# Three output weight pieces converted beside expert 0's first half; VectorE's side work per step set by expert width; first input sums two per step

## The chip, the cores and the metric

The kernel runs on one core of one Trainium2 chip. Its engines are TensorE (PE: matrix products; PEld: the loading of its weights), VectorE (DVE), ScalarE (ACT), GpSimd (POOL) and SyncE (SP, which here only issues DMAs). Each works through its own list of instructions in the order in which the program was written; between engines, semaphores hold an instruction until what it reads is there or what it overwrites has been read. The metric is the device time of one execution in microseconds (us), less is better.

## The reference

Three layers follow one another. The numbers of one feed the next.

```
# 1: gated linear attention, 4 batches x 8 heads, 768 steps, head size 48
f = 1 / (1 + exp(-f_logit))
for t in range(768):
    state = f[t] * state + outer(k[t], v[t])
    y[t] = q[t] @ state
# 2: x = y as (3072, 384); 8 experts (384 -> 1024 -> 384), one for each token
logits = normalised(x) @ normalised(expert_emb).T / tau
expert_idx = argmax(logits); gate = softmax(logits)[expert_idx]
out[mask] = gate * (relu(x[mask] @ w1[e]) @ w2[e])         # for each expert e
# 3: "moe2": w_a, w_b 384 -> 1536, w_out 1536 -> 384
result = ((x @ w_a) * (x @ w_b)) @ w_out
```

## The kernel before, in words

**Numbers in two parts.** A product is made with rounded operands, each kept as a high part (`Copy` on ScalarE) and a low part (raw minus high, a subtraction on GpSimd or VectorE), and three products of high and low are summed. So every weight and every intermediate costs ScalarE one pass and VectorE or GpSimd another.

**Stages.** The scan of the attention runs in 24 groups (`g`) until about 120 us; its inputs q, k, f come through four buffers `qkf0` to `qkf3`. Tokens are scattered to memory by expert (`slots`) with indirect DMAs on GpSimd's queue. Then the first 224 tokens of expert 0 are worked off in the **early stage** (`early_h`, `early_y`, `early_split`, lines 521 to 541, 127 to 145 us) while the rest of the routing is counted on VectorE. Then comes the **expert loop**, `for s in range(64)` with `e, j = divmod(s, 8)`: step s makes one eighth of expert e's hidden layer (`h_part`, products on lines 1212 to 1214, split into `hh` on ScalarE, line 1235, and `hl` on VectorE, line 1236) and adds the eighth before it to the output (`y_part(s - 1)`, line 1255). An expert is 224, 448, 432, 416, 408, 400, 392 or 384 tokens wide (e = 0 to 7). In steps j = 3 to 5 the rows of the next expert are transposed (`x_turn`, TensorE line 1202, then ScalarE line 1205 and VectorE line 1206). The loop ends at about 381 us; after it layer 3 runs in "visits" (lines 1461 to 1494) to about 808 us.

**Side work in the expert loop.** Layer 3's weights come in 64-bit form and are made into 32-bit floats, 18 pieces of 128 x 768 in `conv()`: load (line 925), `Abs` on ScalarE (948), four bit operations on VectorE (950, 951, 954 and 957 or 987). The six pieces of `w_out` are then split (ScalarE 963, GpSimd 964) and stored to the scratch array `wost` (SP, line 969); the twelve of `w_a` and `w_b` are summed into combined blocks in `combine()` (VectorE 999, 1000; ScalarE 1032; GpSimd or VectorE 1035) and stored to `wst` (SP, line 1055). The order of pieces (`waiting`) is three of `w_out`, six of `w_a`, six of `w_b`, three of `w_out`. The experts' own weights are split as they come (`w_more`: ScalarE 886 and 892, two thirds of the low part on GpSimd and one third on VectorE, 887 and 895). From step 58 on the first input sums of layer 3 are made too (`x_first`: VectorE 1347 and 1355, ScalarE 1360).

**What sets the order.** Nothing reorders instructions when the program runs: each engine's list is the order in which the loop calls its parts. `prep_run(s, us)` hands out side work in each step until the costs that its generators yield (estimates written in the code, in us of VectorE) have used up `us`: 1.4 in expert 0, 2.1 later. A step calls `h_part`, `prep_run`, `w_more`, `x_turn` and `y_part(s - 1)` in that order, so VectorE's `hl` of a step stands behind the side work of the step before it.

**Buffers.** When the first stage ends, its pools are closed (`actx.close()`), and the space is given to new ones: `big` (9216 columns, which holds the six buffers `part[0]` to `part[5]` of `conv`), the hidden layer's `hid` pool (`hh`, `hl`), and `yT`. `rows1`, the rows of expert 1, lies in `yT[2]`. They are loaded by SP (line 463), as the first of SP's DMAs after the early stage; behind it on SP stand `w2` weights of an expert (line 130), the first three loads of `conv` (line 925) and the rows of expert 2.

## Time and profile before

| | |
|---|---|
| median of 3 runs | 813.92 us (813.72 to 816.1) |
| profiled execution, its own time | 815.84 us |
| its span | 813.8 us (so 2.04 us lie around the span) |
| PE busy / PEld busy | 769.0 us (95%) / 738.7 us |
| DVE, ACT, POOL busy | 603.7, 420.5, 411.6 us |
| DMA over the span | 226.82 MB, mean 279 GB/s |
| stages on PE | scan to about 120 us, early stage to 145, expert loop to 381, layer 3 to 808 |

How to read it: the profile's page gives busy times by engine and the span in 40 slices; the waits list what TensorE stood for; a timeline gives the instructions of one engine in order, with the idle time ahead of one and what ended it in brackets. PEclk 1.00 is TensorE's full speed.

### The profile page before, as it was taken

To read this page: it belongs to the slowest core of one execution; us is meant where nothing else is said; L and a number is where in the kernel's file an instruction comes from. 1 tells how busy PE (TensorE), PEld (TensorE's weight loads), DVE (VectorE), ACT (ScalarE), POOL (GpSimd) and SP (SyncE) were. 2 spreads that over 40 slices of the span, in tenths; PEclk is the share of its full clock that TensorE was granted. 3 is DMA by queue.
4 is the path that set the end of the run, shared out by engine and by line. 5 is a ranking of instruction groups with operands and counts; after the bars stand their busy time and mean duration, and the time that the engine had idled before them with its cause. 6 is when DMAs were issued, how large, how long until landed. Compare 5 with 4: busy or idle time off the path is not lost.

```text
span 813.8 us, 16794 instructions
## 1 busy us (share of the span) xinstructions
PE 769.0 (95%) x6354; PEld 738.7 (91%) x6354; DVE 603.7 (74%) x1007; ACT 420.5 (52%) x889; POOL 411.6 (51%) x392
## 2 busy tenths in 40 slices
PE   7899989889999899997899999999999999999995
PEld 5799989878998899986798999999999999999994
DVE  6999995589978956787888557856756765786552
ACT  4899974555556646654345344434434434444331
POOL 6667773352377936874255153445326525343313
PEclk9999999999999999999999999999999999999998
DMA  7999852977689975997997998789889888988881
GB/s 272 308 309 319 247 185 92 293 257 236 186 250 284 310 246 170 256 258 230 342 406 288 338 334 321 278 322 335 299 299 325 316 291 313 336 286 306 336 308 64
DMA packets 83088, 226.82 MB, mean 279 GB/s; under 512 B 10650, under 2 KB 42248, under 8 KB 76728
## 3 DMA queue, kind: packets, MB, share of 16 engines
q1 hardware_dynamic: 79639, 216.10, 78.3%
q0 software_dynamic: 3072, 9.56, 3.0%
q8 instruction: 52, 0.85, 0.4%
q14 instruction: 37, 0.30, 0.1%
q10 hardware_dynamic: 288, 0.02, 0.0%
HBM read 192.95 MB, written 32.70 MB: 277 GB/s over the span
## 4 chain that ended last, share of the span: by engine, by line
PE 40%; DVE 8%; DMA 3%; issue 1%; POOL 1%; ACT 1%; SPq 0%; DVEq 0%; POOLq 0%; ACTq 0%
PE pv L1461 21%; PE pw L1461 5%; PE pq L1492 5%; PE pq L1490 5%; PE pq L1494 5%; DMA w<-wst 3%; DVE a L1355 2%; DVE big L1438 2%; DVE big L1477 2%; DVE big L1471 1%; DVE w L1355 1%; POOL out L1523 0%; POOL big L964 0%; DVE big L1474 0%; PE po L1255 0%
## 5 line engine op out<-in xcount | busy, mean ns | idle before, releaser
L1443 POOL TENSOR_TENSOR w<-big,w 128x512 fp32r<-128x512 f32 x72 | 94.2, 1322 | 173.8 <-ACT w L1442 169.6
L1461 PE MATMUL pv<-w,w 128*128 128x256 f32 x912 | 135.6, 283 | 7.0 <-DMA w<-wst 2.4
L1477 DVE TENSOR_TENSOR big<-big,pv 128x512 f32<-128x512 f32 x144 | 98.2, 682 | 58.5 <-PE pv L1461 58.3
L1461 PEld LDWEIGHTS pv<-w,w 128*128 128x128 f32 x912 | 126.3, 189 | 11.5 <-DVE big L1477 3.8
L1461 PE MATMUL pv<-a,w 128*128 128x256 f32 x816 | 120.3, 281 | 0.6 <-DVE big L1471 0.3
L1461 PEld LDWEIGHTS pv<-a,w 128*128 128x128 f32 x816 | 113.5, 188 | 2.4 <-DVE big L1471 1.4
L895 POOL TENSOR_TENSOR w<-raw,w 128x512 fp32r<-128x512 f32 x48 | 78.5, 1654 | 48.1 <-ACT w L892 45.4
L1494 PE MATMUL pq<-raw,w 128*128 128x384 f32 x288 | 97.2, 338 | 1.6 <-POOL w L1443 1.6
L1490 PE MATMUL pq<-raw,w 128*128 128x384 f32 x288 | 97.4, 338 | 0.0
L1492 PE MATMUL pq<-raw,w 128*128 128x384 f32 x288 | 96.9, 337 | 0.0
L1255 PE MATMUL po<-hh,w 128*128 128x224 f32 (+7 forms) x384 | 82.0, 348 | 7.4 <-ACT hh L1235 6.9
L1471 DVE TENSOR_TENSOR big<-big,pv 128x256 f32<-128x256 f32 x96 | 40.3, 420 | 50.5 <-PE pv L1461 48.7
L1255 PEld LDWEIGHTS po<-hh,w 128*128 128x128 f32 x384 | 67.1, 191 | 10.1 <-ACT hh L1235 7.9
L1438 DVE TENSOR_TENSOR big<-big 128x512 f32<-128x512 f32 x72 | 66.1, 946 | 1.6
L1212 PE MATMUL ph<-a,w 128*128 128x224 f32 (+7 forms) x192 | 66.5, 346 | 0.0
L1214 PE MATMUL ph<-a,w 128*128 128x224 f32 (+7 forms) x192 | 66.3, 345 | 0.0
L1213 PE MATMUL ph<-a,w 128*128 128x224 f32 (+7 forms) x192 | 66.3, 345 | 0.0
L1442 ACT ACTIVATE w<-big 128x512 fp32r<-128x512 f32 x72 | 44.8, 633 | 38.5 <-DVE big L1438 38.5
L1468 ACT ACTIVATE big<-pw 128x256 f32<-128x256 f32 x48 | 18.3, 382 | 77.7 <-PE pw L1461 77.7
L1235 ACT ACTIVATE hh<-ph 128x224 fp32r<-128x224 f32 (+7 forms) x64 | 31.3, 490 | 52.0 <-PE ph L1214 51.8
L1494 PEld LDWEIGHTS pq<-raw,w 128*128 128x128 f32 x288 | 54.3, 189 | 2.2 <-POOL w L1443 2.2
L1490 PEld LDWEIGHTS pq<-raw,w 128*128 128x128 f32 x288 | 54.3, 189 | 0.6 <-ACT w L1442 0.6
(275 smaller groups left out, 1738.2 us busy)
## 6 DMA issues: line engine op xcount, KB each, us to landing
w<-wst SPq DMA_DIRECT2D x49, 1024.0 KB, 7.3
w<-wst SPq DMA_DIRECT2D x49, 896.0 KB, 6.1
raw<-wost SPq DMA_DIRECT2D x72, 384.0 KB, 7.1
raw<-moe_w SPq DMA_DIRECT2D x32, 768.0 KB, 6.8
qkf<-qkf SPq DMA_DIRECT2D x20, 768.0 KB, 5.1
wst<-big SPq DMA_DIRECT2D x21, 512.0 KB, 7.3
vx<-vx SPq DMA_DIRECT2D x24, 192.0 KB
big<-moe_w_out SPq DMA_DIRECT2D x6, 768.0 KB
```

Of the source, the lines that this page charges most:

```text
L895: (G if i < NPOOL else V).tensor_tensor(out=wt[:, 1, f], in0=raw[:, f], in1=wt[:, 0, f].bitcast(F32), op=ALU.subtract)
L1212: T.matmul(out=out, lhsT=wh, rhs=xh, start=first, stop=False)
L1213: T.matmul(out=out, lhsT=wl, rhs=xh, start=False, stop=False)
L1214: T.matmul(out=out, lhsT=wh, rhs=xl, start=False, stop=last)
L1255: T.matmul(out=OS[e][k], lhsT=w[:, j % 4, k * 128:(k + 1) * 128], rhs=x, start=(j == 0 and w is wh and x is hh), stop=(j == FJ - 1 and x i ...
L1438: V.tensor_tensor(out=a, in0=a, in1=b, op=ALU.mult)
L1443: G.tensor_tensor(out=g[:, 1], in0=a, in1=g[:, 0].bitcast(F32), op=ALU.subtract)
L1461: T.matmul(out=out, lhsT=wt, rhs=xt_, start=first and j == 0, stop=j == 2, skip_group_check=True)
L1477: V.tensor_tensor(out=o, in0=o, in1=bank, op=ALU.subtract)
L1490: T.matmul(out=q, lhsT=gh, rhs=wh, start=(f == 0), stop=False)
L1492: T.matmul(out=q, lhsT=gh, rhs=wl, start=False, stop=False)
L1494: T.matmul(out=q, lhsT=gl, rhs=wh, start=False, stop=(f == F2J - 1))
```

## The change

The instructions of TensorE are the same 5901 in the same order. What moves are the lists of the other engines.

1. Three of the six `w_out` pieces (c = 0, 2, 4) are loaded by SP in groups 20, 21 and 22 of the scan into `qkf0`, `qkf1`, `qkf2`, which are free by then (`pre_load`), and converted by `pre()`, a generator that is called by `pre_step` between the parts of the early stage: per piece ScalarE `Abs`, VectorE four operations (max, shift, two bit operations), ScalarE `Copy`, GpSimd subtraction, and two stores to `wost` issued on **GpSimd's** queue. The results lie in `qkf3`, `qkf0`, `qkf1`.
2. `conv` keeps 15 pieces: `w_a`, `w_b`, then three of `w_out`. The first three loads are pieces of `w_a`. The last operation of a `w_a` piece is one of 128 x 3 x 256 instead of three of 128 x 256 (`yT` is one tile now). The late `w_out` results lie in tiles of expert 7's input, and their conversion starts 8 places after the load instead of 3.
3. `rows1` lies in the first columns of `big`.
4. `prep_run` gets `prep_share(s)`, worked out from the expert's width, from what VectorE has in the step anyway, and carries an overdraft to the next step (`debt`). The costs yielded by `conv` and `combine` are changed a little.
5. `w_more(s)` is called ahead of `h_part(s)`, VectorE's third of the weights' low part behind `prep_run`.
6. `x_first` makes two sums a step from s = 57 (three a step from s = 58 before), and one each at the first two places of layer 3.

```
+        pre_to = {0: 3, 2: 0, 4: 1}
+        def pre_load(i):
+            src = I["moe2_w_out"].bitcast(I32).rearrange("(j p) d -> p j d", p=128)[:, 4 * i:4 * i + 2, :]
+            raw = qkf_t[i].rearrange("p c a b -> p (c a b)").bitcast(I32)
+            SP.dma_start(out=raw.rearrange("p (j f) -> p j f", j=2), in_=src)
+        def pre():
+            ct = Bt_all.rearrange("p i a b -> p (i a b)")[:, 0:768]
+            for i in range(3):
+                c = 2 * i
+                ...
+                A.activation(out=ct, in_=r1.bitcast(F32), func=ACTF.Abs)
+                V.tensor_scalar(out=ct, in0=ct, scalar1=C0, scalar2=None, op0=ALU.max)
+                yield
+                V.tensor_scalar(out=ct.bitcast(I32), in0=ct.bitcast(I32), scalar1=3, scalar2=0x3fffffff, ...)
+                yield
+                V.scalar_tensor_tensor(out=r0, in0=r0, scalar=29, in1=ct.bitcast(I32), ...)
+                yield
+                V.scalar_tensor_tensor(out=r0, in0=r1, scalar=-1073741824, in1=r0, ...)
+                to = qkf_t[pre_to[c]].rearrange("p c a b -> p (c a b)").rearrange("p (i j d) -> p i j d", i=2, j=2)
+                src = r0.bitcast(F32).rearrange("p (j d) -> p j d", j=2)
+                A.activation(out=to[:, 0].bitcast(F32R), in_=src, func=ACTF.Copy)
+                G.tensor_tensor(out=to[:, 1].bitcast(F32R), in0=src, in1=to[:, 0], op=ALU.subtract)
+                for h in range(2):
+                    G.dma_start(out=wost[2 * c:2 * c + 2, :, h].rearrange("j p d -> p j d"), in_=to[:, h])
+                yield
...
+            if 20 <= g <= 22:
+                pre_load(g - 20)
...
         early_split(3)
+        pre_step(1)
...
         early_split(7)
+        pre_step(2)
         late_turn()
+        pre_step(1)
         early_y(6)
+        pre_step(2)
...
-        yT = [sp.tile([128, max(sum(CAPS), NT + DM)], F32, name=f"yT{k}") for k in range(KC)]
-        rows1 = yT[2][:, NT - 4 * RW:NT].rearrange("p (j w) -> p j w", j=4)
+        yTs = sp.tile([128, KC, max(sum(CAPS), NT + DM)], F32, name="yT")
+        yT = [yTs[:, k] for k in range(KC)]
+        rows1 = big[:, 0:4 * RW].rearrange("p (j w) -> p j w", j=4)
...
-        waiting = [(w, c) for w in (2, 0, 1, 2) for c in ((0, 2, 4) if w == 2 else range(6))]
-        waiting[-3:] = [(2, 1), (2, 5), (2, 3)]
+        waiting = [(w, c) for w in (0, 1) for c in range(6)] + [(2, 1), (2, 5), (2, 3)]
...
+            us += debt[0]
...
+            debt[0] = min(us, 0)
...
+        def prep_share(s):
+            e, j = divmod(s, FJ)
+            turning = 3 <= j <= 5 and e + 1 < NE
+            us = 18 * max(0.111, 0.000457 * n_of(e)) + (1.0 if turning else 0.0)
+            return PREP * us - 0.56 * (1 + turning + (j == 0)) - 1.2 * len(vlow) - (2.0 if s >= IDS else 0.0)
...
         for s in range(NE * FJ):
             e, j = divmod(s, FJ)
+            w_more(s)
             h_part(s)
...
-            prep_run(s, 1.4 if s < FJ else 2.1)
-            w_more(s)
+            prep_run(s, prep_share(s))
+            while vlow:
+                vlow.pop(0)()
...
-            if s == IDS + 1:
+            if s == IDS:
                 x_more()
-            if s > IDS:
-                for _ in range(3):
+            if s >= IDS:
+                for _ in range(2):
                     next(x_first, None)
```

ScalarE at the end of the early stage, before: `he` are the early halves, `a0` the late rows of expert 0 turned, `sq_junk` the squares of rows, `hh` the hidden layer of step 0.

```order
L525 ACTIVATE he00_155<-u_ps_151 128x224 [waits DVE_49,PE_49]
L525 ACTIVATE he10_157<-y_ps_152 128x224 [waits DVE_49,PE_49]
L501 ACTIVATE a0_88<-u_ps_151 128x224 [waits DVE_49,PE_49]
L501 ACTIVATE a0_88<-ph_2276 128x224 [waits PE_49]
L501 ACTIVATE a0_88<-px_2474 128x224 [waits PE_49]
L541 ACTIVATE rows_84<-kv_2242 128x224 [waits DVE_49,PE_49]
```

ScalarE at the same place now; `Bt` holds the magnitudes, `qkf` the pieces and their high parts.

```order
L568 ACTIVATE Bt_150<-qkf1_147 128x768 [waits DMAHW5_49]
L526 ACTIVATE he00_155<-u_ps_151 128x224 [waits PE_49]
L526 ACTIVATE he10_157<-y_ps_152 128x224 [waits PE_49]
L581 ACTIVATE qkf0_146<-qkf1_147 128x768 [waits DVE_49,Pool_49]
L568 ACTIVATE Bt_150<-qkf2_148 128x768 [waits DMAHW7_49]
L502 ACTIVATE a0_88<-u_ps_151 128x224 [waits PE_49]
L502 ACTIVATE a0_88<-ph_2279 128x224 [waits PE_49]
L502 ACTIVATE a0_88<-px_2497 128x224 [waits PE_49]
L581 ACTIVATE qkf1_147<-qkf2_148 128x768 [waits DVE_49,Pool_49]
L542 ACTIVATE rows_84<-kv_2245 128x224 [waits PE_49]
```

Line 501 before is line 502 now. Behind the third `Abs` stand the late turn and the third `Copy`, and the eviction to `rows` comes behind that. The first `hh` follows after three more instructions.

SP, before, from the load of expert 1's rows (`slots` to `yT2`); DMAHW and DMASW are semaphores of DMAs that SP and GpSimd issued.

```order
L463 DMA yT2_2534<-slots_70 112x1576 [waits DVE_49,DMAHW7_49,PE_49,Pool_49]
L130 ISA
L130 DMA raw_2564<-moe_w2 128x4x384 [waits DMAHW1_49,DMAHW0_49]
L925 DMA big_2525<-moe2_w_out 128x2x768 [waits DMAHW3_49,DMAHW2_49,Pool_49]
L925 DMA big_2525<-moe2_w_out 128x2x768 x2
```

SP at that place now.

```order
L464 DMA big_2555<-slots_70 112x1576 [waits DMASW5_49,DMASW4_49,DMAHW2_49,DMASW3_49,DMAHW3_49,DMASW2_49,DMAHW4_49,DMASW1_49,DMAHW5_49,DMASW0_49,DMAHW7_49,PE_49,Pool_49]
L131 ISA
L131 DMA raw_2592<-moe_w2 128x4x384
L983 DMA big_2555<-moe2_w_a 128x3x512 x2
L983 DMA big_2555<-moe2_w_a 128x3x512 [waits DMAHW6_49]
```

The load of expert 1's rows goes to `big` and waits for six DMAs of GpSimd's queue, which it did not wait for before. The loads behind it are in the same order, with pieces of `w_a` in place of pieces of `w_out`.

VectorE in steps 58 and 59, before: 1236 is `hl`, 999 a combined block, 895 the low part of expert weights, 1347 and 1355 the sums of layer 3's input.

```order
L1236 SCALAR_TENSOR_TENSOR hl<-ph,hh 128x384
L999 TENSOR_TENSOR big<-big 128x512 x2
L1347 TENSOR_TENSOR rows<-yT_2533,yT_2534 128x256
L1347 TENSOR_TENSOR rows<-yT_2532,rows 128x256
L1347 TENSOR_TENSOR rows<-yT_2532 128x256
L1347 TENSOR_TENSOR rows<-rows 128x256
L1355 TENSOR_TENSOR w_66<-rows,w_66 128x256 x2
L1347 TENSOR_TENSOR rows<-yT_2532,yT_2534 128x256
L1236 SCALAR_TENSOR_TENSOR hl<-ph,hh 128x384
L999 TENSOR_TENSOR big<-big 128x512 x2
L895 TENSOR_TENSOR w_65<-raw,w_65 128x512
```

VectorE at the same steps now (1295 is `hl`, 1405 and 1413 the sums, 936 the low part of weights).

```order
L1295 SCALAR_TENSOR_TENSOR hl<-ph,hh 128x384
L1413 TENSOR_TENSOR w_66<-rows,w_66 128x256
L1405 TENSOR_TENSOR rows<-yT 128x256
L1413 TENSOR_TENSOR w_66<-yT,w_66 128x256
L1405 TENSOR_TENSOR rows<-yT,rows 128x256
L1295 SCALAR_TENSOR_TENSOR hl<-ph,hh 128x384
L936 TENSOR_TENSOR w_65<-raw,w_65 128x512
```

The combined blocks are gone from these steps (they are done before step 57), and the sums stand in smaller lots between two `hl`.

## Rows read from the trace of the kernel before

**Rows 1.** The page: busy time by engine, and TensorE's granted clock in 40 slices.
```profile
PE 769.0 (95%) x6354; PEld 738.7 (91%) x6354; DVE 603.7 (74%) x1007; ACT 420.5 (52%) x889; POOL 411.6 (51%) x392
...
PEclk9999999999999999999999999999999999999998
```

**Rows 2.** TensorE's waits: what it waited for, total, times, longest.
```profile
PE po L1255 <- ACT hh L1235: 6.9, 3, 4.0
PE pt L1202 <- DVE a L1206: 5.4, 2, 2.8
PE po L1255 <- DVE hl L1236: 4.6, 4, 1.8
```

**Rows 3.** TensorE's timeline: start, duration, instruction, idle before and what ended it.
```profile
147.02 0.93 PE L1255 MATMUL po<-hh,w 128*128 128x224 f32 x6
...
158.78 0.60 PE L1202 MATMUL pt<-ident,yT 112*128 112x112 f32 x4 [2.67 <-DVE a L1206]
...
260.49 0.83 PE L1255 MATMUL po<-hl,w 128*128 128x416 f32 x3 [1.77 <-DVE hl L1236]
...
283.26 0.71 PE L1202 MATMUL pt<-ident,rows 100*128 100x100 f32 x4 [2.77 <-DVE a L1206]
...
363.69 1.32 PE L1255 MATMUL po<-hh,w 128*128 128x384 f32 x6 [1.90 <-ACT hh L1235]
...
371.14 1.37 PE L1255 MATMUL po<-hh,w 128*128 128x384 f32 x6 [4.03 <-ACT hh L1235]
```

**Rows 4.** SP's timeline: the load of expert 1's rows.
```profile
145.19 0.33 SPq L463 DMA_DIRECT2D yT<-slots  x1
```

**Rows 5.** ScalarE's timeline, early stage and the loop's first steps.
```profile
133.12 0.36 ACT L525 ACTIVATE he<-u_ps 128x224 fp32r<-128x224 f32 x1 [1.53 <-PE u_ps L521]
...
146.63 0.81 ACT L1235 ACTIVATE hh<-ph 128x224 fp32r<-128x224 f32 x2
...
154.85 0.90 ACT L948 ACTIVATE ct<-big 128x768 f32<-128x768 f32 x1 [3.16 <-DMA big<-moe_w_out]
...
161.76 0.90 ACT L963 ACTIVATE big<-big 128x768 fp32r<-128x768 f32 x1 [2.10 <-DVE big L957]
```

**Rows 6.** VectorE's timeline: the bit operations of the first pieces.
```profile
155.79 0.56 DVE L950 TENSOR_SCALAR ct<-ct 128x768 f32<-128x768 f32 x1 [3.67 <-ACT ct L948]
...
158.95 1.78 DVE L954 SCALAR_TENSOR_TENSOR big<-big,ct 128x768 int32<-128x768 int32 x1
160.76 0.96 DVE L957 SCALAR_TENSOR_TENSOR big<-big 128x768 int32<-128x768 int32 x1
...
163.48 1.54 DVE L950 TENSOR_SCALAR ct<-ct 128x768 f32<-128x768 f32 x1 [0.93 <-ACT ct L948]
```

**Rows 7.** GpSimd's timeline: scatters, low parts of weights, low part of a piece.
```profile
133.85 0.97 POOL L475 DMA_INDIRECT slots<-xb,posi  x1 [0.30 <-ACT he L525]
135.12 0.97 POOL L475 DMA_INDIRECT slots<-xb,posi  x1 [0.30 <-issue]
...
156.87 3.04 POOL L887 TENSOR_TENSOR w<-raw,w 128x512 fp32r<-128x512 f32 x2 [5.31 <-ACT w L886]
162.73 1.88 POOL L964 TENSOR_TENSOR big<-big 128x768 fp32r<-128x768 f32 x1 [2.82 <-ACT big L963]
```

**Rows 8.** DMA issues from 100 to 160 us: last number is us from issue to landing.
```profile
slots<-xb,posi POOLq DMA_INDIRECT x14, 3.3
```

**Rows 9.** Windows: length, busy by engine (instructions), granted clock, DMA share, GB/s.
```profile
280.00:300.00 20.00, 17.23 (x88) 16.80 (x87) 13.90 (x19) 9.82 (x18) 8.27 (x6) 0.91 0.83 267
360.00:380.00 20.00, 14.07 (x70) 12.98 (x69) 18.48 (x35) 9.60 (x23) 11.89 (x6) 0.91 0.66 163
380.00:450.00 70.00, 63.20 (x452) 59.07 (x451) 57.37 (x97) 30.68 (x65) 27.61 (x24) 1.00 0.92 348
```

**Rows 10.** Windows from one hl to the next, at steps 35 and 59.
```profile
277.02:283.12 6.10, 3.47 (x20) 3.13 (x18) 6.07 (x6) 5.29 (x10) 5.46 (x4) 1.00 0.89 295
363.67:371.12 7.45, 3.41 (x18) 3.09 (x18) 7.27 (x11) 3.31 (x7) 5.10 (x3) 1.00 0.52 147
```

More of the change, by code (lines that the diff above doesn't have):

```diff
@@ L40 @@
 LAG_N = 3
+PREP = 1.05
 NPOOL = 2
@@ L821, in build @@
         V.tensor_copy(srt[:, 0, 0:1], pcs[:, 0:1])
+        pre_step(1)
         early_h(6)
@@ L879, in job_load, with w_low @@
                 loaded.append((s, n, c, raw))
+        vlow = []
+        def w_low(i, wt, raw, f):
+            op = lambda eng: eng.tensor_tensor(out=wt[:, 1, f], in0=raw[:, f], in1=wt[:, 0, f].bitcast(F32), op=ALU.subtract)
+            if i < NPOOL:
+                op(G)
+            else:
+                vlow.append(lambda: op(V))
         def job_run(n, c, raw):
@@ L886, in job_run @@
                     A.activation(out=wt[:, 0, f], in_=raw[:, f], func=ACTF.Copy)
-                    (G if i < NPOOL else V).tensor_tensor(out=wt[:, 1, f], in0=raw[:, f], in1=wt[:, 0, f].bitcast(F32),
-                                                          op=ALU.subtract)
+                    w_low(i, wt, raw, f)
                     if i < 2:
@@ L894, in job_run @@
                 f = slice(i * 512, (i + 1) * 512)
[L895 to L896 removed]
+                w_low(i, wt, raw, f)
         blocks = lambda t: (lambda m, k: t(k)[:, m * 512:(m + 1) * 512])
@@ L935, in loads @@
                 conv_load(part[i], *waiting[0])
-                ready.append((now[0] + 3, i) + waiting.pop(0))
+                ready.append((now[0] + (3 if now[0] < NE * FJ else 8), i) + waiting.pop(0))
         def take(i, n):
@@ L941, in conv @@
         def conv():
-            for n in range(18):
+            for n in range(15):
                 while not ready or now[0] < ready[0][0]:
@@ L977, in conv @@
                 else:
-                    for k in range(KC):
-                        if w == 1 and k:
-                            continue
-                        if w == 0:
-                            one = lambda t: t[:, k * 256:(k + 1) * 256]
-                            o = wfs[0](k)[:, c * 256:(c + 1) * 256].bitcast(I32)
-                        else:
-                            one = lambda t: t.rearrange("p (k f) -> p k f", k=KC)
-                            o = big[:, 0:KC * FF2].bitcast(I32).rearrange("p (k f) -> p k f", k=KC)[:, :, c * 256:(c + 1) * 256]
-                        V.scalar_tensor_tensor(out=o, in0=one(r1), scalar=-1073741824, in1=one(r0),
-                                               op0=ALU.bitwise_and, op1=ALU.bitwise_xor)
+                    one = lambda t: t.rearrange("p (k f) -> p k f", k=KC)
+                    if w == 0:
+                        at = NT + DM - FF2 + c * 256
+                        o = yTs[:, :, at:at + 256].bitcast(I32)
+                    else:
+                        o = big[:, 0:KC * FF2].bitcast(I32).rearrange("p (k f) -> p k f", k=KC)[:, :, c * 256:(c + 1) * 256]
+                    V.scalar_tensor_tensor(out=o, in0=one(r1), scalar=-1073741824, in1=one(r0),
+                                           op0=ALU.bitwise_and, op1=ALU.bitwise_xor)
                     take(i, 1)
-                yield 0.95
+                yield 1.3
                 if (w, c) == (0, 5):
@@ L1086, in combines @@
             yield from combine(1)
-            free[4] = now[0]
+            free[4] = free[5] = now[0]
             phase[0] = 4
@@ L1544, in build @@
                 y_part(NE * FJ - 1)
+            if at < 2:
+                next(x_first, None)
             while later and later[0][0] <= at:
```

36 lines of the change are left out of this document (26 added, 10 removed).

## The prediction

> **What bounds the kernel now.** I read the page first: TensorE is busy for 769.0 of 813.8 us and its granted clock is near full in every slice [rows 1], and its list of instructions is not touched by the change. So nothing can come of the change but what TensorE waits, and what its clock loses behind a wait. The second view is the list of TensorE's waits: the three largest are for the hidden layer's two parts and the turned rows of the next expert, 6.9 + 4.6 + 5.4 = 16.9 us in nine pieces [rows 2]. Its timeline puts them at their steps [rows 3]: 2.67 us at 158.78 (second expert's rows), 1.77 at 260.49 (step 29), 2.77 at 283.26 (step 36), 1.90 and 4.03 at 363.69 and 371.14 (steps 59 and 60). The rest, 4.6 − 1.77 = 2.8 for `hl` and 6.9 − 1.90 − 4.03 = 1.0 for `hh`, lies in steps 4 to 10. The windows add two things [rows 9]: in 280 to 300 and in 360 to 380 the granted clock is 0.91, that is some 20 x 0.09 = 1.8 us lost behind the stalls just named (the clock stands at 1.2 instead of 2.4 GHz for some us after TensorE stood still); and from 380 to 450, at full clock, TensorE idles for 70 − 63.2 = 6.8 us.
>
> Who is late in these places? Between the `hl` of steps 35 and 36 VectorE is busy for 6.07 of 6.10 us and GpSimd for 5.46, while TensorE has only 3.47 us of work; after the `hl` of step 59 it is 7.27 of 7.45 and 3.41 [rows 10]. VectorE with its side work is the limit of these steps, not the chip's products.
>
> **What is taken away, and its worth.** Fewer and evenly dealt side operations can give back at most what TensorE lost there.
> - Steps 57 to 63: before, two combined blocks, a weight part and up to seven sums stand between two `hl`; now four sums and a weight part, or less. The most is 1.90 + 4.03 + 1.8 = 7.7. I take 7.0, since two sums now stand in front of the first visits of layer 3.
> - Steps 22 to 37: the pieces of `w_out` are gone from the start of the loop, so `w_a`, `w_b` and the blocks move to earlier steps, and the share follows the width. The most is 1.77 + 2.77 + 1.8 = 6.3. By the new lists, at the durations of the trace, steps 22 and 26 carry 8.6 us of VectorE's and GpSimd's work together, where steps 29 and 35 carried 7.7 and 7.3, so I expect new stalls of some 1.5 us there and take 4.8 net (1 to 6.3).
> - Steps 4 to 10: 3.8 at most; the cause, `Copy`, GpSimd's 1.88 us and the fourth bit operation of the `w_out` pieces, is gone. I take 3.8 (2 to 4).
> - Layer 3's start: blocks are finished some steps sooner, so the first chunks can be loaded sooner; of 6.8 us only a part waits for DMAs. I take 2.5 (0 to 4).
>
> Sum of the gains: 7.0 + 4.8 + 3.8 + 2.5 = 18.1 us (10 to 22).
>
> **What is added, and its price.** Three pieces must now be converted between 133 and 145 us, where each engine has gaps, but in series. The chain of one piece: `Abs` 0.90 [rows 5], two operations of 0.56 and two of 0.96 on VectorE [rows 6], `Copy` 0.90 [rows 5]: 4.84 us. The pieces share one buffer for the magnitudes, so they follow one another: 3 x 4.84 = 14.5, from 133.4, behind the `he` of 133.12 [rows 5], where the list puts the first `Abs`. Between the parts stand the early stage's own operations on ScalarE and VectorE (splits, weight parts, counts, the late turn); laid out by the order with their durations they push the chain by 5.1 us. And twice the first VectorE operation of a piece meets GpSimd's subtraction of the piece before. What that does is in the rows: the maximum takes 0.56 us alone but 1.54 at 163.48 under GpSimd's 1.88 us at 162.73, and the bit operation 1.78 against 0.96 under the weight parts of 156.87 [rows 6, 7]. I count 1.5 for both. So the third `Copy` ends at 133.4 + 14.5 + 5.1 + 1.5 = 154.5; GpSimd's subtraction 1.88 [rows 7] leads to 156.4; its two stores are 1.28 apart (135.12 − 133.85) [rows 7], so the second is issued at 157.7, and with a scatter's 3.3 us from issue to landing [rows 8] it lands at **161.0**. The trace has no store of this shape on this queue: if the chain hides 1.5 us more and a store takes less, 159.5; if a store takes twice as long, or the early stage is pushed further, 163.
>
> The Trainium skill speaks of both prices. Its page "SBUF — State Buffer", section "Who interferes with whom", says that a VectorE operation with two inputs in SBUF, or in a two-port mode, and a GpSimd one that reads SBUF exclude each other, the later one standing fully still; the trace agrees (1.54 against 0.56 above), and by it the conversion beside GpSimd's subtractions is dearer than the sum of its parts. "DMA: Bandwidth & Descriptors", section "Anatomy of one DMA — SWDGE (gpsimd) path", gives about 2.0 us plus bytes over 436e3 per us; for a store of 393,216 bytes that is an estimate of 2.9, and the landing would be 0.4 us earlier than by the scatter's row.
>
> Who waits for that landing? `big`, where expert 1's rows now go, and the `hid` pool lie on the space of the buffers that the stores read, and the lists show it: SP's load of the rows waits for all six stores, which it did not before, and so does the first `hh`. Two prices follow.
> - The first `hh` ran at 146.63 and `y_part(0)` began at 147.02 [rows 5, 3]. Now it begins at 161.0 + 0.4 = 161.4: 14.4 us later.
> - The rows' load went out at 145.19 [rows 4], the first `Abs` of the loop ran at 154.85, when its piece had come [rows 5], 9.66 us on, and with it in ScalarE's list ahead of the turned rows TensorE went on at 158.78 [rows 3], 3.93 later. The same queue now starts at 161.0: 161.0 + 9.66 + 3.93 = 174.6, that is **15.8** later than before. This is the larger, and holds the smaller in it. With the bounds for the landing, 14.3 to 17.8; the standstill of 9 us ahead of 161.4 may cost a stretch of half clock too, but it lies ahead of the second wait and is covered by it.
>
> Costed at nothing: the three loads during the scan (SP has little to do there; were they to delay the inputs of a group, it would be some of a 5-us load), the one operation of 128 x 3 x 256 for three smaller ones, and `rows1` in another place but for its wait.
>
> **Sum.** 813.8 + 15.8 − 18.1 = 811.5 for the span; with the 2.04 around it 813.5 for an execution like the profiled one, which stands 1.92 above the median. Against the median: 813.92 + 15.8 − 18.1 = **811.6 us**. A large bill at expert 0 that is paid back later, all but in full.
>
> **The rivals.**
> - All side work fits (0.18): no new stalls in steps 22 to 26, all of the first bounds and more of layer 3's start come back, 7.7 + 6.3 + 3.8 + 4 = 21.8, plus 0.7 of small waits; the wait stays at 14.3 to 15.8. 813.92 + 15.3 − 22.5 = 806.7. For it: the shares are dealt by width, and steps 57 to 63 are far lighter. Against it: the work that moves forward meets steps like those in which VectorE was full [rows 10].
> - VectorE and GpSimd take turns elsewhere (0.25): the denser steps 22, 26 and 30 each stall like steps 29 and 36 did, 1.77 to 2.77 us, and one or two with 1.8 of clock, 9 us together; the gains shrink to 18.1 + 1.5 − 9 = 10.6. 813.92 + 16 − 10.6 = 819.3, slower. From 3.8 us in these steps together the kernel is slower than before (18.1 + 1.5 − 3.8 = 15.8), from 6.2 by over 0.3%; it is the mechanism of [rows 6]. For it: both engines full [rows 10]. Against it: the new budget subtracts what VectorE has to do.
> - The landing of the stores doesn't bind so late (0.09): the conversion hides in the gaps, no operation is blocked and the stores land at about 157; then the wait costs 12, and 813.92 + 12 − 18.1 = 807.8.
>
> **How the numbers follow.** The forecast has 0.48; its own range is 808 to 815, from the bounds of the landing and of each gain. The range of 8 in 10 reaches from 804, below the two quicker rivals, to 820, just past the slower one. A measurement of this kernel tells some 0.3%, 2.4 us, from no change, so faster is below 811.5, slower above 816.4. The forecast lies on the first bound: half of it (0.24) is faster, nearly half (0.22) the same, 0.02 slower; the first and third rival are faster but for a little (0.24 of 0.27, the rest the same), the second mostly slower (0.22 of 0.25, the rest the same). Together faster 0.48, same 0.28, slower 0.24.
>
> **What would show it.** Right: TensorE stands still from about 152 to 161 ahead of the first `po<-hh`, the wait put down to `hh` or a DMA of GpSimd's queue; SP's load of the rows of expert 1 goes out at 159.5 to 163; the third turn of expert 1's rows at 173 to 178; the waits of steps 59 and 60 are gone, and those at 260 and 283 are smaller or replaced by one near step 22 or 26. Wrong: if the first `po<-hh` starts within 5 us of 147, the stores don't gate it and the gain is some 10 us larger; if VectorE is busy from `hl` to `hl` in steps 22 to 30 with TensorE idle for over 6 us, the second rival holds; if the loop's second half keeps its waits, the change doesn't lighten it and it ends near 825.

## The result and the profile after

The changed kernel takes 827.05 us (median of 4 runs, 824.5 to 827.8) against 814.27 for the kernel before on the same chip: ratio 1.0147, 95% interval 1.012 to 1.0175. It is slower by 12.8 us where 2.3 less were forecast. The profiled execution took 827.04 us with a span of 825.3.

The page of the changed kernel, against [rows 1]: each engine is busy for about as long as before. TensorE's work is the same, 6354 matmuls in the same order in both traces. Of the 11.5 us by which the span grew, 8.8 are idle time of TensorE (813.8 - 769.0 before, 825.3 - 771.7 now), and 2.7 are the same matmuls taking longer, behind stalls, at the lower clock.

```profile
PE 771.7 (94%) x6354; PEld 740.8 (90%) x6354; DVE 596.7 (72%) x995; ACT 420.3 (51%) x889; POOL 410.0 (50%) x398
...
PEclk9999999799999999999999999999999999999999
```

TensorE's waits, against [rows 2] (total, times, longest). The one for `hh` has a piece of 7.9 us, and the turned rows are no longer among the largest (one piece of 1.52 below). The wait for `w<-wst`, layer 3's blocks, is about as long as before; the last line has it in the kernel before.

```profile
PE po L1314 <- ACT hh L1294: 10.9, 3, 7.9
PE po L1314 <- DVE hl L1295: 5.0, 5, 1.7
PE pv L1527 <- DVE big L1543: 3.1, 4, 0.9
PE pv L1527 <- DMA w<-wst: 2.6, 1, 2.6
```
```profile
PE pv L1461 <- DMA w<-wst: 2.4, 3, 1.6
```

The same waits at their places, TensorE's timeline, against [rows 3].

```profile
160.88 0.95 PE L1314 MATMUL po<-hh,w 128*128 128x224 f32 x3 [7.89 <-ACT hh L1294]
...
174.11 0.60 PE L1261 MATMUL pt<-ident,big 112*128 112x112 f32 x4 [1.52 <-DVE a L1265]
...
262.43 1.06 PE L1314 MATMUL po<-hh,w 128*128 128x416 f32 x2 [2.41 <-ACT hh L1294]
...
281.58 0.65 PE L1314 MATMUL po<-hl,w 128*128 128x416 f32 x2 [1.66 <-DVE hl L1295]
...
362.70 0.62 PE L1314 MATMUL po<-hl,w 128*128 128x392 f32 x2 [1.58 <-DVE hl L1295]
...
411.31 0.59 PE L1527 MATMUL pv<-w,w 128*128 128x256 f32 x3 [2.57 <-DMA w<-wst]
```

At expert 0 the bill came as it was worked out. ScalarE's third `Copy`, GpSimd's subtraction and stores behind it, and ScalarE's first `hh`, which a DMA of the stores released:

```profile
153.21 0.89 ACT L581 ACTIVATE qkf<-qkf 128x768 fp32r<-128x768 f32 x1 [4.28 <-DVE qkf L577]
...
160.33 0.36 ACT L1294 ACTIVATE hh<-ph 128x224 fp32r<-128x224 f32 x1 [4.58 <-DMA wost<-qkf]
```

```profile
154.19 1.83 POOL L582 TENSOR_TENSOR qkf<-qkf,qkf 128x768 fp32r<-128x768 f32 x1 [3.44 <-ACT qkf L581]
155.98 1.45 POOL L585 DMA_DIRECT2D wost<-qkf  x2
```

SP's load of expert 1's rows, against [rows 4]:

```profile
160.55 0.34 SPq L464 DMA_DIRECT2D big<-slots  x1
```

How long did a store take? The profile lists the six of them with 3.6 us in the median from issue to landing, as far as it could follow them:

```profile
wost<-qkf POOLq DMA_DIRECT2D x6, 384.0 KB, 3.6
```

By the same measure the scatters had 3.3 [rows 8], so the row that the forecast took was 0.3 short. The estimate of 2.9 us by the Trainium skill's page "DMA: Bandwidth & Descriptors", section "Anatomy of one DMA — SWDGE (gpsimd) path", is 0.7 short of this measure; from the end of the two issues (155.98 + 1.45 = 157.4) to `hh` at 160.33 are 2.9 us too, so it depends on where one starts to count.

**Where the time came from.** TensorE executes the same matmuls in the same order, so the start of one matmul after, less its start before, says how far the kernel has fallen back by that point. I call this the shift. It is read from the two timelines at the matmuls that started at the given times before; a step in it is a loss or a gain between two places. Each line below is one kernel; the names are those of the experiments further down. The ratio is to the kernel before on the same chip; kernels that ran on different chips are better compared by it than by their medians.

```
us in the kernel before:   159   207   277   364   381   794   median  ratio [95%]
changed kernel            15.3   9.6  18.5  14.8   8.8  11.5   827.05  1.0147 [1.0120, 1.0175]
e1_nopre                   2.0   2.6  10.9   6.3   0.1  26.6   838.72  1.0285 [1.0268, 1.0303]
e2_preonly                17.7  12.0  12.7   7.6   6.1   4.0   821.12  1.0083 [1.0064, 1.0102]
e3_flat                   19.1  13.8  25.1  20.3  17.1  19.2   831.00  1.0194 [1.0177, 1.0211]
e4_order                  17.2  11.5  20.4  15.1   9.5  12.3   826.20  1.0127 [1.0098, 1.0156]
f1_wfirst                 16.3  11.3  21.6  17.1  14.6  12.4   826.45  1.0150 [1.0102, 1.0198]
f2_share                  16.2  10.5  19.8  13.6   9.8  18.4   830.61  1.0197 [1.0147, 1.0246]
f3_sums                   16.2  10.5  10.8   5.3   1.5  -1.9   816.08  1.0021 [0.9995, 1.0046]
f4_onetile                14.4   8.6  10.2   4.4   2.9   0.5   817.74  1.0046 [1.0025, 1.0067]
g0_sumsonly                0.8   0.8   0.6   2.2   2.2   0.8   816.07  1.0008 [0.9990, 1.0026]
g1_onepiece                4.8   3.0   4.2   4.6  -1.7   6.6   822.21  1.0075 [1.0054, 1.0095]
g3_nogate                 17.2  10.8  15.6  10.9   7.4   3.3   817.99  1.0018 [0.9997, 1.0039]
g4_two                    10.0   6.8   7.6   3.2  -1.2   3.0   818.23  1.0041 [1.0025, 1.0056]
h1_loadbehind             15.6  10.8  16.0  15.7  13.2  10.7   828.70  1.0182 [1.0159, 1.0205]
h5_loadahead              15.2   9.5  19.6  15.7  14.4  10.9   827.33  1.0162 [1.0142, 1.0181]
h3_oldlate                16.1  10.4  19.2  15.0   9.0  14.3   828.49  1.0159 [1.0137, 1.0180]
h4_all                     6.7   0.5   1.1  -3.5  -7.0 -11.0   808.55  0.9926 [0.9903, 0.9948]
j1_afterpools              7.3   0.8  10.7   6.4   0.4   2.4   819.36  1.0069 [1.0043, 1.0094]
j2_noearly                -0.7  -1.0  -1.2  -1.4  -1.1  -2.2   813.65  1.0000 [0.9986, 1.0013]
```

In the first line: 15.3 are lost at expert 0 and 5.7 come back by 207; then 8.9 are lost up to 277, 3.7 come back by 364 and 6.0 by 381, and layer 3 costs 2.7. The loss between 207 and 277 stands where the forecast put a gain. Three windows of the changed kernel divide it, from the `hl` of step 22 to that of 26, on to that of 27, and on to that of 31 (columns: TensorE, its weight loads, VectorE, ScalarE, GpSimd busy, instructions; clock, DMA share, GB/s):

```profile
238.92:253.17 14.25, 12.55 (x65) 11.71 (x64) 14.11 (x15) 7.46 (x11) 11.87 (x8) 1.00 1.03 240
253.17:262.52 9.35, 5.91 (x35) 5.31 (x34) 3.54 (x6) 3.56 (x5) 1.77 (x2) 0.97 0.95 314
262.52:280.94 18.42, 16.88 (x82) 15.91 (x82) 18.25 (x20) 11.38 (x23) 16.00 (x10) 0.92 0.92 262
```

In the first and the third VectorE is full, as in [rows 10]: 14.11 of 14.25 us and 18.25 of 18.42. In the second it works for 3.54 of 9.35 us, so it isn't the limit there, it waits. Up to 242 us of the kernel before, in the first, the shift rises by 2.2 us (9.6 to 11.8); up to 250, with the wait of the second and the stretch of half clock behind it, by 5.3 (to 17.1); up to 277, in the third, by the rest (to 18.5). For whom VectorE waits in the second, three timelines say. VectorE waits for ScalarE's `Abs` (`ct`):

```profile
259.46 0.56 DVE L1008 TENSOR_SCALAR ct<-ct 128x768 f32<-128x768 f32 x1 [5.71 <-ACT ct L1006]
```

ScalarE waited for a DMA before that: the high part of a block (line 1087) may overwrite its buffer only when the block before it in that buffer has been stored (`wst<-big`). The split of expert weights (line 952), which the change moved ahead, stands between it and the `hh` that TensorE waits for at 262.43.

```profile
256.66 0.63 ACT L1087 ACTIVATE big<-yT 128x512 fp32r<-128x512 f32 x1 [4.83 <-DMA wst<-big]
258.54 0.89 ACT L1006 ACTIVATE ct<-big 128x768 f32<-128x768 f32 x1 [1.25 <-DMA big<-moe_w_b]
260.48 1.48 ACT L952 ACTIVATE w<-raw 128x1536 fp32r<-128x1536 f32 x1 [1.05 <-DMA raw<-moe_w]
261.87 0.50 ACT L1294 ACTIVATE hh<-ph 128x416 fp32r<-128x416 f32 x1
```

And SP, which issues these stores, has the load of expert weights (line 930) ahead of them now. Behind it the stores go out in a heap: three issues take 7.33 us together, then two 3.56.

```profile
247.13 0.38 SPq L930 DMA_DIRECT2D raw<-moe_w  x1
247.61 7.33 SPq L1110 DMA_DIRECT2D wst<-big  x3
257.41 0.38 SPq L930 DMA_DIRECT2D raw<-moe_w  x1
257.89 3.56 SPq L1110 DMA_DIRECT2D wst<-big  x2
```

### The profile page after: what moved, and what is told of

Its sections match the earlier page's. It is cut to its first block, busy times and chain, and to the rows that moved or that the text cites. A ratio compares the mean times of both kernels' runs of the same rounds, so it can differ in the third digit from the quotient of the medians.

```text
span 825.3 us, 16763 instructions
## 1 busy us (share of the span) xinstructions
PE 771.7 (94%) x6354; PEld 740.8 (90%) x6354; DVE 596.7 (72%) x995; ACT 420.3 (51%) x889; POOL 410.0 (50%) x398
## 4 chain that ended last, share of the span: by engine, by line
PE 52%; DVE 26%; DMA 9%; issue 5%; POOL 3%; ACT 3%; SPq 0%; ACTq 0%; DVEq 0%; POOLq 0%
PE pv L1527 21%; PE pw L1527 5%; PE po L1314 5%; PE pq L1556 5%; PE pq L1560 5%; PE pq L1558 5%; DVE Rt L242 3%; DVE Bt L231 3%; DVE qc L250 2%; DMA raw<-moe_w 2%; DMA big<-moe_w_b 2%; DVE big L1543 2%; DVE a L1413 2%; DVE big L1504 2%; DMA qkf<-qkf 2%
## 5 line engine op out<-in xcount | busy, mean ns | idle before, releaser
L936 POOL TENSOR_TENSOR w<-raw,w 128x512 fp32r<-128x512 f32 x56 | 83.8, 1517 | 69.3 <-ACT w L952 46.1
L1295 DVE SCALAR_TENSOR_TENSOR hl<-ph,hh 128x224 fp32r<-128x224 f32 (+7 forms) x64 | 35.5, 555 | 45.5 <-ACT hh L1294 45.5
```

Source lines behind the costliest of these rows:

```text
L936: op = lambda eng: eng.tensor_tensor(out=wt[:, 1, f], in0=raw[:, f], in1=wt[:, 0, f].bitcast(F32), op=ALU.subtract)
```

## The experiments

Each was built from the kernel before or the changed one; the table above has what was measured. First, which edit costs what.

**e1_nopre**, the changed kernel without early conversion (it leaves out the delay of the late `w_out` pieces, which may then overwrite some of the first input sums, so it shows where TensorE waits and isn't a kernel to use):

```
-            if 20 <= g <= 22:
-                pre_load(g - 20)
...
-            for _ in range(n):
-                next(pre_ops, None)
...
+        waiting = [(w, c) for w in (2, 0, 1, 2) for c in ((0, 2, 4) if w == 2 else range(6))]
...
+            us += 1.3 if 4 <= s < 20 else 0.0
```

> The changed kernel without the early conversion: the three w_out pieces go back to the front of the loop's conversions, expert 1's rows lie in yT again; the width-dealt shares get 1.3 us more in steps 4 to 19 for the three pieces, the late pieces' delay is 3 as before. Theory G (the wait for the stores is a loss of 15 us that the rest never earns back): the first po<-hh at 146 to 148 instead of 160.9, and the whole 10 to 15 us below the changed kernel's 827, so 812 to 817. Rival B (the loss lies in the new dealing of side work in steps 16 to 40): the first po<-hh is early as well, but the stalls of the changed kernel between 230 and 300 us return in full (9 us) and layer 3's start loses again, so that it stays above 819.

**e2_preonly**, the kernel before with early conversion (parts 1 and 3 of the change and, of part 2, the 15 pieces in their new order) and nothing else:

```
+        def pre_load(i):
...
...
+        rows1 = big[:, 0:4 * RW].rearrange("p (j w) -> p j w", j=4)
...
+        waiting = [(w, c) for w in (0, 1) for c in range(6)] + [(2, 1), (2, 5), (2, 3)]
```

> The kernel before plus the early conversion alone (15 pieces left in the loop, expert 1's rows in big), with the old flat shares, the old order of the weights' split and the old first sums. Theory G: first po<-hh at 160 to 162; from the shift of 15 only the small stalls of steps 4 to 10 come back (4 to 5 us), and up to 6 in steps 58 to 60 since the combined blocks end at step 53: 819 to 825. Rival B: the early conversion is not what hurts; the loop with three pieces less and old shares earns back 12 or more, 814 to 818.

**e3_flat**, the changed kernel with the old shares and costs; **e4_order**, the changed kernel with `w_more` behind the side work again:

```
-            prep_run(s, prep_share(s))
+            prep_run(s, 1.4 if s < FJ else 2.1)
```
```
-            w_more(s)
             h_part(s)
...
+            w_more(s)
```

> The changed kernel with the old shares: 1.4 us in expert 0, 2.1 later, no overdraft, the old costs. Theory B (whole pieces, four bit operations, now fall into one step, at steps 22, 26, 30, and hold up hl and hh): with the old shares the pieces are spread over two steps again, the stalls between 240 and 300 us shrink from 10 to under 5, and the time falls by 4 to 8 to 819 to 823. Rival O (the stalls come from the weights' split ahead of hh in ScalarE's list, waiting for its DMA): no change within 2 us, 825 to 829.

> The changed kernel with the experts' weight split behind the side work again (as before the change), VectorE's list as in the changed kernel. Theory O: the wait for hh at 262 us (2.4 us, then 1.7 of half clock) goes, the x_turn and output waits beside it too, so 4 to 6 us less: 821 to 823. Rival B: within 2 us of the changed kernel, 825 to 829.

The shift at 159 is 2.0 without early conversion and 17.7 with it alone: the wait at expert 0 belongs to it. The loss from 207 to 277 doesn't: e1_nopre has it (8.3), e2_preonly has 0.7. And neither of its two candidates is alone in making it: without the new shares it is 11.3, without the new order 8.9. Each must be enough by itself, and the next pair asks that the other way round, with one edit added to e2_preonly. In e1_nopre, layer 3 stands 15.86 us for its first blocks, which end only in step 61: without early conversion the new loop is too late at its end. Of the expectations, that of e2_preonly's first theory held (819 to 825), e1_nopre stayed above 819 as its rival said, e3_flat (831.00) lies above both of its ranges, and e4_order fits its rival.

**f1_wfirst** (e2_preonly plus part 5) and **f2_share** (e2_preonly plus part 4):

```
+            w_more(s)
             h_part(s)
...
+            while vlow:
+                vlow.pop(0)()
```
```
-            prep_run(s, 1.4 if s < FJ else 2.1)
+            prep_run(s, prep_share(s))
```

> The kernel before with the early conversion (821.1 us by itself), and of the other parts only the weights' split moved ahead of the hidden layer's product. Theory O (ScalarE stands for the split's DMA ahead of hh, between 240 and 280 us): the shift against the kernel before, 12.7 us at 277 in the early conversion alone, rises to 18 to 22, and the time to 826 to 829. Rivals B and T (shares; one tile for the turned rows): 820 to 822, shift 12 to 14.

> The kernel before with the early conversion, and of the other parts only the shares by width with overdraft and the new costs. Theory B (whole pieces fall into steps 22, 26, 30): the shift at 277 rises from 12.7 to 17 to 20, time 825 to 828. Rivals O and T: 820 to 822.

Both lose: 10.3 and 9.3 us from 207 to 277, as the two theories had it (f2_share's time is above its range). In f2_share VectorE is the limit, as the second rival had it: it is busy for 23.45 of 25 us while TensorE idles nearly 7, and the bit operation of 0.96 us takes 2.03 at 260.05. In e3_flat, the new order with the old shares, it is busy for 18.21 of the same 25 us: there the loss is made without a full VectorE.

```profile
260.00:285.00 25.00, 18.17 (x89) 16.63 (x88) 23.45 (x26) 13.42 (x25) 15.70 (x10) 0.95 0.92 277
```

In f1_wfirst it is SP's list or the splits. **h5_loadahead** (first diff) adds to e2_preonly the load ahead alone, **h1_loadbehind** (second diff; `w_more` there is without its `job_load`) the splits alone:

```
+            job_load(s)
             h_part(s)
```
```
+            w_more(s)
             h_part(s)
...
             prep_run(s, 1.4 if s < FJ else 2.1)
+            job_load(s)
```

> The opposite half: early conversion alone, only the load of the weights (SP) ahead of the hidden layer, the splits behind the side work as before. Theory A (SP's list): stalls come between 207 and 277 us as in f1_wfirst, 7 to 10 us, time 825 to 828. Theory B (splits on ScalarE and GpSimd): no more than 2 us there, time 820 to 823.

> Early conversion alone plus the splits of the experts' weights ahead of the hidden layer (as f1_wfirst), but the load of the weights (SP) goes back behind the side work. Theory A, SP's list decides: in f1_wfirst the load stood ahead of the step's stores, waited for its buffer and let the stores out in bursts. Then the 10 us that f1_wfirst lost between 207 and 277 us of the kernel before go, TensorE's shift there stays within 3 us, and the time is 819 to 823 us. Theory B, ScalarE and GpSimd are late because the splits stand ahead of hh and hl: the loss stays at 7 to 10 us and the time is 825 to 828.

The load alone makes the loss whole: 9.5 to 19.6. Without it the splits still cost 5.2, more than the 3 that theory A allowed; ScalarE waits there for the load that now comes later (3.40 us for `raw<-moe_w` at 258.50). h1_loadbehind's time missed too (828.70), since it loses 6.1 us more from 317 (11.5) to 347 (17.6), where it waits 2.50 for `hh` and then runs at half clock for a stretch. So SP's order is enough for the whole loss, and the place of the splits makes some of it too. What SP waited for, from 200 to 285 us, in e2_preonly and then in h5_loadahead (total, times, longest; line 928 loads expert weights, 1103 stores blocks):

```profile
SPq L1103 <- POOL big L1083: 15.2, 12, 2.1
SPq L928 <- DVE w L945: 9.7, 5, 5.3
```

```profile
SPq L928 <- DVE w L945: 27.5, 8, 7.4
SPq L1103 <- POOL big L1083: 2.9, 4, 1.0
```

In e2_preonly SP waits most for the blocks that it is to store. In h5_loadahead it stands at loads whose buffer VectorE still reads, up to 7.4 us, and finds the blocks behind them ready. There isn't more to move: the share of the DMA engines from 230 to 290 us is 0.98 in the one and 0.95 in the other. SP in e2_preonly and in h5_loadahead, in the same steps:

```profile
243.96 1.89 SPq L1103 DMA_DIRECT2D wst<-big  x3
248.62 0.38 SPq L928 DMA_DIRECT2D raw<-moe_w  x1
249.67 0.38 SPq L1103 DMA_DIRECT2D wst<-big  x1
251.81 0.41 SPq L973 DMA_DIRECT2D big<-moe_w_b  x1
253.04 0.36 SPq L1103 DMA_DIRECT2D wst<-big  x1
```

```profile
247.07 0.38 SPq L928 DMA_DIRECT2D raw<-moe_w  x1
247.50 3.64 SPq L1103 DMA_DIRECT2D wst<-big  x2
251.24 3.53 SPq L973 DMA_DIRECT2D big<-moe_w_b  x1
256.39 0.38 SPq L928 DMA_DIRECT2D raw<-moe_w  x1
256.82 4.78 SPq L1103 DMA_DIRECT2D wst<-big  x3
```

In the first, issues take 0.4 to 0.9 us, and most stores lie apart. In the second they follow the load at once, and issues take up to 3.53 us. ScalarE pays, in h5_loadahead:

```profile
261.52 0.63 ACT L1080 ACTIVATE big<-yT 128x512 fp32r<-128x512 f32 x1 [4.36 <-DMA wst<-big]
```

**The small parts.** **f3_sums** is e2_preonly with two sums per step, **f4_onetile** e2_preonly with one bit operation for three, **g0_sumsonly** the kernel before with two sums per step:

```
-            if s > IDS:
-                for _ in range(3):
+            if s >= IDS:
+                for _ in range(2):
                     next(x_first, None)
```
```
+        yTs = sp.tile([128, KC, max(sum(CAPS), NT + DM)], F32, name="yT")
+                        o = yTs[:, :, at:at + 256].bitcast(I32)
```

> The kernel before with the early conversion, and of the other parts only the first sums two per step from step 57. All theories: same as the early conversion alone up to step 57; then the wait of 1.3 us at 376 and those about 383 to 387 (2.8 together) go, 1 to 4 us less, 817 to 820.

> The kernel before with the early conversion, and of the other parts only the turned rows in one tile, with one operation of 128 x 3 x 256 per piece of w_a. Theory T (something waits for the whole tile): the shift at 277 rises from 12.7 to over 17, time 824 to 828. Rivals O and B: 820 to 822.

> The kernel before with the first sums two per step from step 57 and nothing else of the change. If the gain of the sums (5 us beside the early conversion) needs the early conversion (which ends the combined blocks at step 53), the stalls of steps 59 and 60 stay for the most part, since the blocks still stand there: 811 to 815. If the sums alone do it: 807 to 810.

On top of early conversion the sums give 5.0 us and the single operation 3.4 (3.0 by the ratios), both more than was expected; in the kernel before, the sums give nothing. Its trace still has the combined blocks in steps 57 to 59 and stalls of 1.76 and 3.43 us behind them.

**Getting rid of the wait at expert 0.** **g1_onepiece** converts one piece early, with `rows1` in its old place, **g3_nogate** three with the conversion's buffers in a pool of their own (and the copy of expert 0's output and the rows of expert 2 asked for at step 5), **g4_two** the same with two pieces; all have f3_sums' edit:

```
+        q_p = actx.enter_context(tc.tile_pool(name="q", bufs=1))
-        qkf_t = [ob_p.tile(...)
+        qkf_t = [q_p.tile(...)
```

> The kernel before, the sums two per step, and only ONE piece converted in the early stage (its store lands about 148), two left in the loop, expert 1's rows in the turned rows' tile. Theory G (the wait for the third piece's stores is what costs at expert 0): the first po<-hh at 147 to 150 instead of 160 to 163, the blocks end at step 56, so the stalls of 59 and 60 go too; 803 to 809. Rival (the early conversion costs because it displaces work, not because its stores are waited for): 812 to 816, like three pieces with the sums (816.1).

> All three pieces early, the sums two per step, old shares and order, and the buffers of the conversion in a pool of their own under tiles that are needed late, so that neither the first hh nor expert 1's rows wait for the stores (the copy of expert 0's early half and the load of expert 2's rows move to step 5). Theory G: the first po<-hh at 155 to 158 (behind the third Copy in ScalarE's list, 5 us less than with the wait), expert 1's rows go out before 150, the turn at 164 to 169; 806 to 811 against 816.1 with the wait. Rival (the wait hides behind the conversion anyway): 814 to 817.

> As the kernel without the wait, but with two pieces early and one in the loop. Theory: what is left of the loss at expert 0 is the third piece's chain in ScalarE's and VectorE's lists; with two pieces the first po<-hh comes at 149 to 152; 803 to 808, under one piece and three. Rival: no better than three without the wait, 806 to 811.

All three missed: 803 to 811 us were expected, and they took 822.21, 817.99 and 818.23. One piece costs only 4.8 at 159, two cost 10.0, but layer 3's start then loses 8.3 and 4.2; why was not settled. In g3_nogate `hh` is free and the wait stands one place on. VectorE's copy of the tokens' numbers (`ids`), whose pool still lies on the same space, waits for the stores:

```profile
167.02 0.18 DVE L1243 COPY ids<-rows 112x20 f32<-112x20 f32 x1 [8.05 <-DMA wost<-qkf]
```

**h4_all** puts `ids` and `ct` into a pool that lies elsewhere, and takes f3_sums' and f4_onetile's edits; **j2_noearly** is its control, both edits without early conversion; **j1_afterpools** is the changed kernel whole with the pools of h4_all and, like it, the rows of expert 2 asked for at step 5.

```
+        sp2 = ectx.enter_context(tc.tile_pool(name="small", bufs=1))
+        ids = [sp2.tile([HP, 4, XO], F32, name=f"ids{i}") for i in range(2)]
+        ct = sp2.tile([128, 768], I32, name="ct")
```

> Old order and old shares; early conversion with its buffers in a pool of their own, the small tiles (ids, magnitudes of the loop) in another, the rows of expert 2 asked for at step 5, first sums two per step, one bit operation for three. In g3_nogate the wait for the six stores had only moved to the copy of ids (8.05 us). If that was the last operation gated by them, TensorE's shift after expert 0 is 11 to 13 instead of 17, and with the sums (-5) and the single operation (-3) the time is 808 to 813, faster than before. Rival, the next one gated is the turn of expert 1's rows (its tile a2 still lies on the buffers) as late as ids was: shift 16 to 18, time 814 to 817.

> The kernel before with the first sums two per step and one bit operation for three, without early conversion: the control for h4_all (808.55 us). If the early conversion is what pays there (it takes three pieces out of the loop's start, so that the blocks end before the sums begin), this one is 812 to 815. If the sums and the single operation alone pay, it is 806 to 810.

> The changed kernel whole, with only what gates expert 0 taken away: the conversion's buffers in a pool of their own, ids and the loop's magnitudes in another, the rows of expert 2 asked for at step 5. Theory, the wait for the stores and the loss in steps 22 to 37 are two separate bills: TensorE's shift is 1 to 4 us at 186 us of the kernel before (10.0 in the changed kernel), the 8 to 9 us between 207 and 277 stay, and the time is 815 to 819 us. Rival, the loss in steps 22 to 37 follows from the late start (side work bunched behind it): it goes too, and the time is 806 to 811.

h4_all beats both kernels: 808.55 us, ratio 0.9926 [0.9903, 0.9948], with a smaller loss at expert 0 than its theory had (6.7 at 159, not 11 to 13). Its wait for `hh` is 3.06 us, and 6.7 at 159 have shrunk to 0.5 at 207:

```profile
154.98 0.56 PE L1304 MATMUL po<-hh,w 128*128 128x224 f32 x1 [3.06 <-ACT hh L1284]
```

Its waits in all: of [rows 2], `hh` is 4.3 (6.9 before), `hl` 2.8 (4.6), and the turned rows are no longer among the eleven largest.

```profile
PE po L1304 <- ACT hh L1284: 4.3, 3, 3.1
PE po L1304 <- DVE hl L1285: 2.8, 5, 0.9
```

Without early conversion the same edits give nothing, 1.0000 [0.9986, 1.0013], and j2_noearly still has the stalls of steps 59 and 60:

```profile
357.68 0.44 PE L1253 MATMUL po<-hh,w 128*128 128x384 f32 x1 [1.76 <-ACT hh L1233]
...
370.32 0.69 PE L1253 MATMUL po<-hl,w 128*128 128x384 f32 x1 [3.41 <-DVE hl L1234]
```

j1_afterpools answers whether the two bills are one. Its shift is 0.8 at 207, yet it loses 9.9 us up to 277 (the changed kernel 8.9), in the same place (2.41 us for `hh`), and is slower than before (819.36, just above its theory's 815 to 819). The loss in steps 22 to 37 is not a consequence of the late start.

```profile
255.03 0.71 PE L1317 MATMUL po<-hh,w 128*128 128x416 f32 x1 [2.41 <-ACT hh L1297]
```

**h3_oldlate**, the changed kernel with the late `w_out` pieces as before, asks after layer 3's start:

```
-                    to = flat(X[NE - 1][(n + 1) % 2]).rearrange("p (i j d) -> p i j d", i=2, j=2)
+                    to = part[5].bitcast(F32R).rearrange("p (i j d) -> p i j d", i=2, j=2)
-                ready.append((now[0] + (3 if now[0] < NE * FJ else 8), i) + waiting.pop(0))
+                ready.append((now[0] + 3, i) + waiting.pop(0))
```

> The changed kernel with the three late pieces of w_out handled as before: results in the sixth buffer, conversion 3 places behind the load, so that one load of them, not two, stands ahead of layer 3's first chunks on SP. Theory, the two loads and the stores at the start of layer 3 cost the 4 to 5 us that layer 3 lost from 381 to 429: time 821 to 824, and the 2.6 us that TensorE waits for the chunk w<-wst go. Rival, the chunks are late because DMA is shared with the blocks' stores: no change, 825 to 828.

The theory failed. Layer 3 waits longer for its blocks, 4.9 us instead of 2.6, and the time is no better.

```profile
PE pv L1527 <- DMA w<-wst: 4.9, 2, 4.3
```

## Why the prediction was wrong, point by point

- **The wait at expert 0 was right.** The third `Copy` ended at 153.21 + 0.89 = 154.1 (154.5 predicted), the second store was issued by 157.4 (157.7), both had landed by 160.33 (161.0), the rows' load went out at 160.55, `y_part(0)` began at 160.88 (161.4) and the third turn at 174.11 (174.6). The shift was 15.3 instead of 15.8.
- **The blocked operations were right.** VectorE's maximum, 0.56 alone, took 1.03 and 1.53 in the second and third piece, beside GpSimd's subtraction; 1.5 was counted for the two, 0.47 + 0.97 = 1.4 came. The subtraction still ran for 0.61 and 1.11 us when they began (it took 1.86 from 140.93 and from 147.49):

```profile
142.18 1.03 DVE L569 TENSOR_SCALAR Bt<-Bt 128x768 f32<-128x768 f32 x1 [1.92 <-ACT Bt L568]
...
148.24 1.53 DVE L569 TENSOR_SCALAR Bt<-Bt 128x768 f32<-128x768 f32 x1 [1.84 <-ACT Bt L568]
```

- **Steps 4 to 10**: 3.8 were expected, 5.7 came back (15.3 to 9.6). For the same matmuls TensorE idled 4.2 us before (158.78 to 207.25) and 1.2 now (174.11 to 216.83), which is 3.0; the other 2.7 is the lower clock of that stretch before (0.96 granted, 1.00 now), which the step didn't count.
- **Steps 22 to 37 are the step that failed**: "I expect new stalls of some 1.5 us there and take 4.8 net (1 to 6.3)". From 207 to 287 the shift rose from 9.6 to 14.0, a loss of 4.4, off by 9.2 us of the 13.8 by which the span missed. One gain was there: the stall of 2.77 at 283 [rows 3] is gone (the shift falls from 18.5 at 277 to 15.6 at 283). The size of the new stalls was wrong, 8.9 us where 1.5 were taken, and they have two causes. One was left out: the prediction costed VectorE's work by step and nothing of what the earlier call of `w_more` (part 5) does to SP's list, where a load that waits for its buffer now stands ahead of stores that ScalarE's buffers wait for; that alone costs 10.1 us (h5_loadahead). The prediction read SP's list for expert 0, and not here. The other was in it, but too small: the new shares (part 4) fill VectorE, and alone they cost 9.3 us (f2_share).
- **The second rival had the place, nearly the size and part of the mechanism.** It said 9 us in steps 22, 26 and 30 with VectorE full; 8.9 came up to 277. In the changed kernel VectorE was full on both sides of the longest stall, and in the stall itself it waited for ScalarE. The two causes don't add: taking out either leaves the loss (8.9 without the new order, 11.3 without the new shares, against 8.9). The rival's 819.3 us was still too low, since it kept the gain at layer 3's start, among others.
- **Steps 57 to 63** gave 6.0 from 364 to 381 where 7.0 were taken; two stalls for `hl` came new, the larger of 1.58 at 362.70.
- **Layer 3's start** was to gain 2.5 and lost 2.7. The blocks were indeed done sooner (last store to `wst` issued at 368.34, before at 373.17), but TensorE waits for them as long as before, 2.6 us against 2.4, at another chunk. From the first matmul of layer 3 to that of 450 us it idles 1.6 us more (8.2 against 6.6), and the same matmuls take 1.4 longer (granted clock 0.87 from 407 to 420, behind the wait at 411.31). This is the second term that was wrong, by 5.2 of the 13.8. The new shares have a part: f2_share loses 8.6 there from 381 to 794, where e2_preonly gains 2.1. h3_oldlate rules out the late pieces' handling. What makes the first chunks late was not settled.
- **The range** of 804 to 820 was narrower than the prediction's own bounds, which reach 813.92 + 17.8 - 10 = 821.7. Even these didn't hold the result.

## What to carry to other kernels

A moved call moves everything that it issues: read the list of each queue anew, and ask of a load that goes ahead of stores whose buffer it waits for and who waits for the stores. Work put into a gap is free only if its buffers are too: h4_all and g3_nogate do the same conversion, and what divides them beside one saved operation is whose pool lies on the buffers that the stores read. A change of several parts should be timed in parts; here early conversion with the two small edits was worth 0.7% (h4_all), and the new order, shares and late pieces on top of it cost some 11 us (j1_afterpools).

## What the runs showed of the hardware that was not expected

- **A DMA's issue on SP is not of fixed length.** A store to `wst` took 0.36 to 0.38 us on SP's sequencer where it stood alone (249.67 and 253.04 in e2_preonly). In a row behind a weights' load, two took 3.64 together and a following load 3.53 alone (h5_loadahead, 247.50 and 251.24). Whatever stands behind them on SP is later by that much. Standing behind a load isn't enough, though: in the same kernel such stores took 0.51 at 215.62 and 0.49 at 223.40, and in the kernel before, with the old order, one took 5.65 at 355.90. What makes an issue long was not measured.
- **TensorE's clock after its standstill.** After the 7.89 us ahead of 160.88 the granted clock of 156 to 167 us was 0.53, near the 1.2 GHz level; the same window before, in which TensorE was busy for 5.92 us, was at 1.00. As predicted it cost nothing more, since it lay ahead of the second wait, of which 1.52 us were left at 174.11.

```profile
156.00:167.00 11.00, 6.12 (x31) 6.15 (x32) 4.07 (x14) 2.52 (x6) 4.91 (x8) 0.53 0.71 229
```
